# Spectral mixing plus gated MLP on one core: product 4 of gate and up joined over both position halves, and a last half block in a PSUM bank of its own

## The chip, the core and the metric

The kernel runs on one core of a Trainium2 chip. A core has TensorE (matrix products into PSUM, eight banks of 512 fp32 columns), VectorE and ScalarE (element by element), GpSimd and SyncE, whose queues here issue DMAs (called POOL and SP in the profile). The metric is the device time of one execution in microseconds, as the median of several runs.

## The reference

Two branches share the input `x` (2048 positions, 512 features) and are mixed by a gate per position:

```python
g = sigmoid((x * gate_w).sum(-1, keepdims=True))
a = Real(DFT_seq(DFT_hidden(x)))        # matrices given: Cr@(x@Wre.T) - Ci@(x@Wim.T)
gate = x @ W_gate; up = x @ W_up        # 512 -> 1792
b = (gate * (gate > 0) * up) @ W_down   # 1792 -> 512
return g * a + (1 - g) * b
```

All is fp32.

## The kernel before

**Precision.** Each fp32 operand is split into a high part (`h`: a ScalarE cast to fp32r) and a low part (`l`: a VectorE subtraction), and each product of tiles is three matmuls, low x high, high x low and high x high (`PARTS`). A matmul is 128x128 weights by 512 columns.

**Stages in order of time.**

1. *Gate/up.* The 14 column tiles of W_gate and W_up are taken in seven column pairs `c`, the positions in two halves `q`. For one `c` and `q` a two by two block product is done by seven products in place of eight (the products 1 to 7 of `LEFT`, `RIGHT`): sums of input blocks on either side, and sums of results. Each of the seven is 2 sides (gate and up, `i`) x 2 k x 3 parts = 12 matmuls, accumulated in PSUM bank pairs `x`, `m`, `y`, `t`. ReGLU makes `h` from them, which is written to HBM (`hd`). Pairs 0 and 1 of half 0 come first; pair 2 runs as two plain `Block`s; pairs 3 to 6 run as `Joined`: there product 2 of both halves together is done by another seven products of one k each (`JointX` makes its right sides once, `JointW` its left sides per pair, `jw`). Pairs 0 and 1 of half 1 are run between the spectral blocks.
2. *Spectral blocks*: x times the hidden DFT matrices, results `a` and sums `as` stored to HBM (`ad`).
3. *Down*, twice (`q` = 0, 1): h times W_down by seven products. `RAW` lists the (half, group of two pairs) whose forms of `h` are summed here (`made`) from four stored blocks; for the others seven forms are stored in stage 1 (`h_sums`) and read here.
4. *Sequence*: 26 products (`TURN`), each 4 parts x 12 matmuls, right sides from the sequence DFT matrices (`r`, `c`), left sides from `ad` (`l`, `w`). `SUMS` tells how operands are summed from others. Some right sums (`FORMED`) are made ahead into HBM (`td`): by DRAM-to-DRAM copies with an accumulating second copy, both issued by POOL (`form_stored`, paced by tokens), or by loads, VectorE sums and stores (`form_rights`, `form_lefts`). Results are summed in PSUM and in SBUF (`js`), gated and accumulated into the output.

**The order of work** is made by a planner at build time. Every step has a key: a time in units of one matmul (0.22667 us). TensorE's steps keep their order; for VectorE and ScalarE the planner takes due times (`due`) and a small model, and fixes one order for each engine; DMA issues stay in the order of their keys. SBUF is 51 units (`UNITS`) of 4 KB per partition, given out by the same plan. `LEAD`, `RAMP`, `FORM_LEAD` and `ahead` shift keys of preparation. `load` issues on SP, `store` and `accumulate` on POOL, and `put` is `load`. All instructions are issued at line 266, so the profile is read by tile names.

**The tail.** In the last turn the products of side `i` = 1, part 3 are done in two halves of 256 columns, both in the same bank; after each, `tail` multiplies by the gate, adds the value stored before, and SP stores the result:

```python
for i, cols, k in ((0, slice(N), 12), (1, HALVES[0], 3), (1, HALVES[1], 0)):
    z = o[:, i, cols]
    op(key - k, lambda z=z, i=i, cols=cols: E().vector.scalar_tensor_tensor(
        z, x[i][:, cols], float(sign), g[:, cols], op0=OP.mult, op1=OP.mult))
    op(key - k, lambda z=z, i=i, cols=cols: combine(z, z, v[:, i, cols], 1))
    op(key - k, lambda z=z, i=i, cols=cols: load(od[t, :, 2 * d + i, cols], z))
```

The functions that the change touches, and what calls them, with the line numbers of the profile:

Of the kernel before, what the change touches and what calls it, by code (L numbers as in the profile page):

```python
# [9 lines left out]
F32R = mybir.dt.float32r  # L10
# [10 lines left out]
UNITS = 51  # L21

# [34 lines left out]
FORMED = (16, 18, 19, 35, 37, 38)  # L57
# [211 lines left out]
class Plan:  # L269
# [47 lines left out]
    def due(self):  # L317

        last, n = {}, self.now
        for s in reversed(self.steps):  # L320
            if s.engine == "tensor" and s.key >= 0:
                n -= 1
            if s.engine == "tensor":
                last[s] = min(last.get(s, 1e9), n * self.MATMUL)
            elif s not in last or s.key > 0:
                last[s] = min(last.get(s, 1e9), (s.key + self.REST) * self.MATMUL)
            s.due = last[s] - (s.work + self.LANDING if s.name == "dma_start" else 0)
            for x in s.after:
                last[x] = min(last.get(x, 1e9), s.due - self.WAIT - (x.work if x.name != "dma_start" else 0))
# [91 lines left out]
def kernel(ctx: ExitStack, tc, xP, xG, wgu, wd, cr, ci, wri, gw, out):  # L421
# [189 lines left out]
    RAW = {(0, 1), (1, 2), (0, 0), (0, 3), (0, 2)}  # L611
# [97 lines left out]
    class Joined(Block):  # L709


        def __init__(self, q, w):
            super().__init__(q, w)
            self.u["11"] = buf("u11")
            if not q:
                self.s[1] = buf("s1")

        def run(self, joint=None):
            slots = {(5, 1): (5, 1), (6, 1): (6,), (3, 0): (3, 7), (3, 1): (2, 4)}
            for m, i in [(m, i) for m in (1, 5, 6) for i in range(2)] + [(3, 0), (7, 0), (3, 1), (7, 1), (4, 0), (4, 1)]:  # L720
# [5 lines left out]
                for y in slots.get((m, i), ()) if joint else ():  # L726
                    joint.step(y)
# [42 lines left out]

    class JointW:


        def __init__(self, w, x, key):
            self.w, self.x = w, x
            raw, s = buf("jws", [4, P]), w.raw[0]
            self.t = buf("jw", [2, 4, P], F32R)
            self.s = {y: buf(f"jv{y}", (N,)) for y in (1, 5, 6)}
            self.o = [buf(f"jo{q}") for q in range(2)]
            op(key - 30, lambda: combine(raw[:, 0], s[:, 1, 0, 1], s[:, 1, 1, 1], 1))  # L780
            op(key - 30, lambda: combine(raw[:, 2], s[:, 1, 0, 0], s[:, 1, 0, 1], -1))
            op(key - 29, lambda: combine(raw[:, 1], raw[:, 0], s[:, 1, 0, 0], -1))
            op(key - 28, lambda: combine(raw[:, 3], s[:, 1, 1, 0], raw[:, 1], -1))
            op(key - 24, lambda: E().scalar.copy(self.t[:, 0], raw.all))
            op(key - 20, lambda: E().vector.tensor_sub(self.t[:, 1], raw.all, f32(self.t[:, 0])))

        def left(self, y, a):
            if y in (1, 2, 4):
                return self.w.a[a][:, 1, int(y > 1), int(y == 4)]
            return self.t[:, a, {5: 0, 6: 1, 7: 2, 3: 3}[y]]  # L790
# [5 lines left out]
        def product(self, y):  # L796
            for n, (a, b) in enumerate(PARTS):
                mm(PAIRS["x"][int(y in (5, 3, 2))], self.left(y, a), self.x.x[y][:, b],
                   start=y in (1, 5, 2) and n == 0, stop=n == 2)

        def evac(self, y, key):
            Y, M = (PAIRS["x"][n] for n in range(2))
            s, o, e = self.s, self.o, E()
            if y in (1, 5, 6):
                op(key, lambda: e.scalar.copy(s[y].all, M if y == 5 else Y))
            elif y == 4:
                op(key, lambda: e.scalar.copy(o[0][:, 1], Y))
            else:
                q, i, ps, t = {3: (1, 0, M, 6), 7: (1, 1, Y, 5), 2: (0, 0, M, 1)}[y]
                op(key, lambda: e.vector.tensor_add(o[q][:, i], ps, s[t].all))  # L810
# [60 lines left out]
    class SpectralBlock:  # L871
# [47 lines left out]
        def out(self, f, key):  # L919
            for j in range(2):  # L920
                n = 2 * PLACE.index(2 * self.q + j)
                o = ad[f, n:n + 2, :, 2 * self.ih:2 * self.ih + 2].rearrange("x p t n -> p x t n")
                op(key, lambda o=o, j=j: store(o, self.o[f"{f + 1}{j + 1}"].all))
            part = {x: self.o[f"{f + 1}{PLACE[x // 2] % 2 + 1}"][:, x % 2] for x in range(8) if PLACE[x // 2] // 2 == self.q}
            mine = [v for v in DIRECT if GROUP[v] == self.q]
            for n, v in enumerate(mine):
                if n % 2 == 0:
                    s = buf("as", (2, 2, HD))
                p, q, sign = signed(*SUMS["l"][v - 8], SIGNS["l"], v)
                y = part[v] = s[:, n % 2]  # L930
                op(key + 2 + 4 * n, lambda y=y, p=part[p], q=part[q], sign=sign: combine(y, p, q, sign))
                op(key + 6 + 4 * n, lambda y=y, v=v: store(ad[f, v, :, 2 * self.ih:2 * self.ih + 2], y))
# [152 lines left out]
    def formed(side, blocks, trails, parts, first, last, source, name, shape):  # L1085
# [4 lines left out]
        for part, trail in chains:  # L1090
            old = None
            for x, v in trail:
                b = buf(name, shape)
                op(key - FORM_LEAD, lambda b=b, x=x, part=part: load(b.all, source(part, x)))
                if old:
                    a, o = old
                    p, q, s = signed(*SUMS[side][v - blocks], SIGNS[side], v)
                    p, q = (o, b) if p == a else (b, o)
                    op(key, lambda o=o, p=p, q=q, s=s: combine(o.all, p.all, q.all, s))
                    op(key + 5, lambda o=o, v=v, part=part: put(source(part, v), o.all))  # L1100
                old = x, b
                key += gap
# [32 lines left out]
    class Sequence:  # L1135
# [79 lines left out]
        def run(self):  # L1215
# [6 lines left out]
            for turn, product in enumerate(TURN):  # L1222
                (rv, rg), (lv, lg), (ov, og) = (SIDE[x][product] for x in "rlo")
                ps, fresh, sign = joins.begin(turn, ov, SIGNS["r"][rv] * rg * SIGNS["l"][lv] * lg * og)
                late = []
                for part in range(4):
                    c = self.split("c", (2, N), *r[turn, part], False)
                    if part % 2 == 0:
                        w = self.split("w", (4, HD), *l[turn, part], sign < 0)
                    if turn < len(TURN) - 1 or part < 2:  # L1230
                        for i in range(2):
                            pe(6, self.product, ps, w, c, part, fresh, i)
                    else:
                        late.append((w, c, part))
                for i, (w, c, part) in sorted(((i, x) for i in range(2) for x in late), key=lambda y: (y[0], y[1][2])):
                    if (i, part) == (1, 3):
                        for cols in HALVES:
                            pe(3, self.product, ps, w, c, part, fresh, i, cols)
                    else:
                        pe(6, self.product, ps, w, c, part, fresh, i)  # L1240
                joins.end(turn, ov)

        def product(self, ps, w, c, part, fresh, i, cols=slice(N)):
            hh = part % 2
            for k in range(2):
                for n, (a, b) in enumerate(PARTS):
                    mm(ps[i][:, cols], w[a][:, 2 * hh + k, i * P:(i + 1) * P], c[b][:, k, cols],
                       start=fresh and part == k == n == 0, stop=part == 3 and k == 1 and n == 2)

    class Joins:  # L1250


        def __init__(self, stage):
# [7 lines left out]
            self.place, self.free, self.late, self.turn = {}, [(Pair(n), -999) for n in range(4)], None, 0  # L1261

# [19 lines left out]
        def begin(self, turn, v, sign):  # L1282
# [6 lines left out]
            if fresh or kind == "s":  # L1289
                p, freed = self.free.pop(0)  # L1290
                if not fresh:
# [9 lines left out]
            return x, fresh, sign * s  # L1301

# [46 lines left out]
        def done(self, v):  # L1349
# [3 lines left out]
            g, key = buf("gg", (N,)), self.at(self.turn + 1)  # L1353
            row = gd[0, KD * t:KD * (t + 1)].rearrange("i p -> (i p)").partition_broadcast(P)
            op(key - 80, lambda: load(g.all, row))
# [12 lines left out]
        def tail(self, x, sign, t, d, g, key):  # L1368
            o, v = buf("z"), buf("v")
            op(key - 100, lambda: load(v.all, od[t, :, 2 * d:2 * d + 2]))  # L1370
            for i, cols, k in ((0, slice(N), 12), (1, HALVES[0], 3), (1, HALVES[1], 0)):
                z = o[:, i, cols]
                op(key - k, lambda z=z, i=i, cols=cols: E().vector.scalar_tensor_tensor(
                    z, x[i][:, cols], float(sign), g[:, cols], op0=OP.mult, op1=OP.mult))
                op(key - k, lambda z=z, i=i, cols=cols: combine(z, z, v[:, i, cols], 1))
                op(key - k, lambda z=z, i=i, cols=cols: load(od[t, :, 2 * d + i, cols], z))

# [87 lines left out]
    def prepared(c, ahead=74):  # L1465
# [4 lines left out]
    for c in range(2, NP):  # L1470
# [10 lines left out]
        else:  # L1481
            pair = [Joined(q, w) for q in range(2)]
# [30 lines left out]
    for n in range(2):  # L1513
# [64 lines left out]
```

## Time and profile before

| | |
|---|---|
| median of 3 runs | 770.4 us (769.77 to 770.6) |
| the profiled execution, its own time | 770.19 us |
| its span, first to last instruction | 768.4 us |
| TensorE busy | 762.5 us, 3360 matmuls |
| VectorE busy | 652.1 us |
| ScalarE busy | 407.1 us |
| mean granted TensorE clock | 0.999 |
| DMA packets, bytes | 60046, 190.16 MB |

Times in rows are microseconds from the start of the span unless marked ns. A timeline row gives start, duration, engine, line, operation, output tile `<-` input tiles, shape, count, and in brackets idle time before it and what ended it. A row of the stretches gives, per engine, busy time and number of instructions (PE, PE weight load, DVE, ACT, POOL), then the clock, the DMA engines' busy share and GB/s. A row of the groups gives total busy time and the mean of one in ns, then idle time before them. A DMA row gives count, KB each, and median us from issue to landing.

### The profile page before, as it was taken

To read this page: it belongs to the slowest core of one execution; us is meant where nothing else is said; L and a number is where in the kernel's file an instruction comes from. 1 tells how busy PE (TensorE), PEld (TensorE's weight loads), DVE (VectorE), ACT (ScalarE), POOL (GpSimd) and SP (SyncE) were. 2 spreads that over 40 slices of the span, in tenths; PEclk is the share of its full clock that TensorE was granted. 3 is DMA by queue.
4 is the path that set the end of the run, shared out by engine and by line. 5 is a ranking of instruction groups with operands and counts; after the bars stand their busy time and mean duration, and the time that the engine had idled before them with its cause. 6 is when DMAs were issued, how large, how long until landed. Compare 5 with 4: busy or idle time off the path is not lost.

```text
span 768.4 us, 9329 instructions
## 1 busy us (share of the span) xinstructions
PE 762.5 (99%) x3360; PEld 629.0 (82%) x3360; DVE 652.1 (85%) x714; ACT 407.1 (53%) x493; POOL 110.0 (14%) x163
## 2 busy tenths in 40 slices
PE   9999999999999999999999999999999999999997
PEld 7888888888888888888888888888888887888886
DVE  6999766738489784989998669999999999979984
ACT  6666444534445354555654535656675455826740
POOL 0122121111110332020000000022110110113020
PEclk9999999999999999999999999999999999999999
DMA  8376897866897989787349898899995997999885
GB/s 320 121 237 158 259 271 212 238 182 189 256 296 270 358 330 333 261 283 260 111 165 348 285 391 253 247 245 228 263 267 186 258 258 251 239 238 282 263 178 109
DMA packets 60046, 190.16 MB, mean 247 GB/s; under 512 B 6752, under 2 KB 7264, under 8 KB 60000
## 3 DMA queue, kind: packets, MB, share of 16 engines
q1 hardware_dynamic: 41776, 124.03, 44.8%
q0 software_dynamic: 18224, 65.54, 37.6%
q8 instruction: 26, 0.43, 0.2%
q14 instruction: 20, 0.16, 0.1%
HBM read 143.65 MB, written 66.86 MB: 274 GB/s over the span
## 4 chain that ended last, share of the span: by engine, by line
PE 96%; DVE 3%; issue 1%; DVEq 0%
PE ps L266 96%; DVE cl L266 1%; DVE wl L266 0%; DVE r L266 0%; DVE js L266 0%; DVE z L266 0%; DVE ps L266 0%; DVE l L266 0%; DVEq L266 0%
## 5 line engine op out<-in xcount | busy, mean ns | idle before, releaser
L266 PE MATMUL ps<-ch,wl 128*128 128x512 f32 x418 | 162.4, 389 | 0.1
L266 PE MATMUL ps<-cl,wh 128*128 128x512 f32 x418 | 162.3, 388 | 0.2 <-DVE cl L266 0.2
L266 PE MATMUL ps<-ch,wh 128*128 128x512 f32 x418 | 162.2, 388 | 0.0
L266 ACT CAST ch<-r 128x1024 fp32r<-128x1024 f32 x104 | 105.9, 1050 | 95.1 <-DVE r L266 67.7
L266 DVE TENSOR_TENSOR cl<-r,ch 128x1024 fp32r<-128x1024 f32 x104 | 124.6, 1221 | 0.4
L266 PEld LDWEIGHTS ps<-ch,wl 128*128 128x128 f32 x418 | 78.5, 188 | 17.0 <-DVE js L266 0.9
L266 PEld LDWEIGHTS ps<-cl,wh 128*128 128x128 f32 x418 | 78.5, 188 | 16.5 <-DVE cl L266 0.6
L266 PEld LDWEIGHTS ps<-ch,wh 128*128 128x128 f32 x418 | 78.5, 188 | 16.3
L266 PE MATMUL ps<-ch,ll 128*128 128x512 f32 x196 | 76.2, 389 | 0.0
L266 PE MATMUL ps<-cl,lh 128*128 128x512 f32 x196 | 76.2, 389 | 0.0
L266 PE MATMUL ps<-ch,lh 128*128 128x512 f32 x196 | 76.2, 389 | 0.0
L266 ACT CAST ch<-hr 128x1024 fp32r<-128x1024 f32 (+1 forms) x56 | 51.3, 943 | 34.8 <-DVE hr L266 20.5
L266 DVE TENSOR_TENSOR cl<-hr,ch 128x1024 fp32r<-128x1024 f32 (+1 forms) x56 | 59.2, 1087 | 9.8 <-ACT ch L266 9.7
L266 ACT COPY s<-ps 128x1024 f32<-128x1024 f32 (+1 forms) x48 | 41.8, 872 | 45.1 <-PE ps L266 44.1
L266 DVE TENSOR_TENSOR u<-ps,s 128x1024 f32<-128x1024 f32 x28 | 34.2, 1220 | 15.6 <-PE ps L266 8.8
L266 DVE TENSOR_TENSOR wl<-l,wh 128x1024 fp32r<-128x1024 f32 x38 | 46.2, 1220 | 0.0
L266 ACT ACTIVATE ps<-ps 128x512 f32<-128x512 f32 (+1 forms) x30 | 23.4, 781 | 43.0 <-PE ps L266 42.2
L266 ACT CAST wh<-l 128x1024 fp32r<-128x1024 f32 x38 | 39.5, 1048 | 11.6 <-DVE l L266 11.2
L266 PE MATMUL ps<-xh,wb0l 128*128 128x512 f32 x112 | 43.7, 390 | 0.0
L266 PE MATMUL ps<-xh,wb0h 128*128 128x512 f32 x112 | 43.6, 389 | 0.0
L266 PE MATMUL ps<-xl,wb0h 128*128 128x512 f32 x112 | 43.6, 389 | 0.0
L266 PE MATMUL ps<-xh,wb1l 128*128 128x512 f32 x112 | 43.6, 389 | 0.0
(147 smaller groups left out, 1504.5 us busy)
## 6 DMA issues: line engine op xcount, KB each, us to landing
l<-ad SPq DMA_DIRECT2D x32, 512.0 KB, 6.8
hr<-hd SPq DMA_DIRECT2D x30, 512.0 KB, 5.4
td<-cr POOLq DMA_DIRECT2D x20, 512.0 KB, 6.0
td<-ci POOLq DMA_DIRECT2D x20, 512.0 KB, 6.3
r<-td SPq DMA_DIRECT2D x20, 512.0 KB, 8.0
wr<-wgu SPq DMA_DIRECT2D x16, 512.0 KB, 8.3
ad<-a POOLq DMA_DIRECT2D x16, 512.0 KB, 6.2
r<-cr SPq DMA_DIRECT2D x16, 512.0 KB, 7.5
```

Of the source, the lines that this page charges most:

```text
L266: getattr(getattr(nc, self.engine), self.name)(*map(ap, self.a), **{k: ap(x) for k, x in self.k.items()})
```

## The change

Four things change.

- Product 4 of column pairs 4, 5 and 6 (`FOURS = 4`) is taken for both halves by seven products, as product 2 was: `JointFour` makes its right sides once, a second `JointW` (with `m=4`) its left sides per pair. The block 21 is then the contents of bank pair `y` minus the joined result (`last`). In half 1, products 6 and 7 use bank pair `t`, and the order of the products changes.
- The last turn's second side is split into two halves of columns for parts 2 and 3, and the last half goes to a spare bank, to which ScalarE copies what was accumulated. For that half, the accumulated block and the right operands are multiplied by the gate, and the stored value is added, before the matmuls (`gate_early`), so that only a copy is left, which ScalarE makes and stores by a DMA that it issues itself (`tail_gated`).
- Right sum 17 is formed ahead (`FORMED`, `form_rights([17], ...)`); the times of the other forming steps, `RAW`, and several leads are new.
- Spectral outputs are stored through SP (`put`), and the formed sums through POOL (`store`). In `due` a matmul counts by its columns.

```diff
+FOURS, FOUR_KEY, FOUR_W = 4, -140, 30
-FORMED = (16, 18, 19, 35, 37, 38)
+FORMED = (16, 17, 18, 19, 35, 37, 38)
-LEAD = {'r': {'load': 44, 'sum': 52, 'sums': 6, 'draws': 30, 'hi': 42, 'lo': 34}, 'l': {'load': 40, 'sum': 62, 'sums': 8, 'draws': 40, 'hi': 55, 'lo': 38}}
-RAMP = 40
-FORM_LEAD = 60
+LEAD = {'r': {'load': 44, 'sum': 60, 'sums': 6, 'draws': 30, 'hi': 42, 'lo': 26}, 'l': {'load': 38, 'sum': 62, 'sums': 6, 'draws': 40, 'hi': 55, 'lo': 34}}
+RAMP = 80
+FORM_LEAD = 46
...
             if s.engine == "tensor" and s.key >= 0:
-                n -= 1
+                n -= s.writes[0].size() / N
...
-    RAW = {(0, 1), (1, 2), (0, 0), (0, 3), (0, 2)}
+    RAW = {(0, 1), (0, 0), (1, 1), (0, 3), (0, 2), (1, 0), (1, 3)}
...
     class Joined(Block):
+            if four and q:
+                self.banks = {**PAIRS, "y": PAIRS["t"]}
...
+            order = [(3, 0), (7, 0), (3, 1), (7, 1), (4, 0), (4, 1)]
+            fours = {}
+            if self.four:
+                slots = {(5, 1): (5, 1), (6, 1): (6,), (7, 0): (3, 7), (3, 0): (2, 4)}
+                fours = {(6, 0): (5, 1), (7, 0): (6,), (7, 1): (3, 7), (3, 0): (2, 4)}
+                order = [(7, 0), (7, 1), (3, 0), (3, 1)]
+            for m, i in [(m, i) for m in (1, 5, 6) for i in range(2)] + order:
                 pe(6, self.product, m, i)
-                if m in (6, 7):
+                if m == 6 or m == 7 and not self.four:
                     self.half(m, i, plan.now)
...
+                for j, some in ((self.four, fours), (joint, slots)) if joint else ():
+                    for y in some.get((m, i), ()):
+                        j.step(y)
+                        if j is self.four and y == 4:
+                            self.last(plan.now)
+                if self.four and not joint and (m, i) == (7, 1):
+                    self.last(plan.now)
+
+        def last(self, key):
+            u, y, o = self.u["21"], self.banks["y"], self.four.o[self.q]
+            op(key + 1, lambda: E().vector.tensor_sub(u.all, y.all, o.all))
+            op(key + 2, lambda: E().vector.scalar_tensor_tensor(
+                self.h[1][:, 0], u[:, 0], 0.0, u[:, 1], op0=OP.max, op1=OP.mult))
...
+    class JointFour:
+        def __init__(self, key):
+            a, b = (X[q, 4][2] for q in range(2))
+            for n, (y, src, f) in enumerate(((5, t5, (b[:, 0], a[:, 0])), (6, t6, (b[:, 1], t5)),
+                                             (7, t7, (b[:, 1], b[:, 0])), (4, t4, (a[:, 1], t6)))):
+                x = self.x[y] = buf(f"kx{y}", dtype=F32R)
+                op(key + 12 * n, lambda src=src, f=f: combine(src, *f, -1))
+                op(key + 12 * n + 4, lambda x=x, src=src: E().scalar.copy(x[:, 0], src))
+                op(key + 12 * n + 8, lambda x=x, src=src: E().vector.tensor_sub(x[:, 1], src, f32(x[:, 0])))
...
     class JointW:
-        def __init__(self, w, x, key):
+        def __init__(self, w, x, key, m=2):
+            raw, s = buf("jws", [4, P]), w.raw[0][:, 1] if m == 2 else w.raw[1][:, 0]
+            self.bank = PAIRS["x" if m == 2 else "t"]
...
-                op(key, lambda o=o, j=j: store(o, self.o[f"{f + 1}{j + 1}"].all))
+                op(key, lambda o=o, j=j: put(o, self.o[f"{f + 1}{j + 1}"].all))
...
-                    op(key + 5, lambda o=o, v=v, part=part: put(source(part, v), o.all))
+                    op(key + 5, lambda o=o, v=v, part=part: store(source(part, v), o.all))
...
+                if turn == len(TURN) - 1:
+                    order[4:] = [(2, 0, slice(N)), (3, 0, slice(N)), *((part, 1, cols) for cols in HALVES for part in (2, 3))]
...
+                    if joins.gated:
+                        op(hi - 1, lambda raw=raw: E().vector.tensor_mul(raw[:, :, HALVES[1]], raw[:, :, HALVES[1]], joins.wide))
...
+                    if (turn, part, i) == (len(TURN) - 1, 2, 0):
+                        joins.spare = joins.free[0][0]
+                        op(plan.now, lambda: E().scalar.copy(ps8[:, joins.spare.n + 1, HALVES[1]], ps8[:, ps.n + 1, HALVES[1]]))
...
+        def gate_early(self, v, x, s, key):
+            op(key - 100, lambda: load(self.v.all, od[t, :, 2 * d:2 * d + 2]))
+            y, z = x[:, :, half], self.v[:, :, half]
+            op(key, lambda: E().vector.tensor_mul(y, y, self.wide))
+            op(key, lambda: combine(y, y, z, s * FLIP_T[t]))
...
+        def tail_gated(self, x, sign, t, d, key):
+            for i, n, k in ((0, 0, 12), (0, 1, 12), (1, 0, 6), (1, 1, 0)):
+                z, y = o[:, i, cols], ps8[:, (x if k else self.spare).n + i, cols]
+                if n:
+                    op(key - k, lambda z=z, y=y: E().scalar.activation(z, y, AF.Copy, scale=float(sign)))
+                else:
+                    op(key - k, lambda z=z, y=y, cols=cols: E().vector.scalar_tensor_tensor(
+                        z, y, float(sign), self.g[:, cols], op0=OP.mult, op1=OP.mult))
+                    op(key - k, lambda z=z, i=i, cols=cols: combine(z, z, self.v[:, i, cols], 1))
+                if i or n:
+                    issue = plan.scalar.dma_start if i and n else load
...
-    form_stored([37, 18, 16, 19], 156, 18)
-    form_stored([35], 788, 30)
-    form_rights([38], 784, 1330)
+    form_stored([16, 37, 18], 150, 11)
+    form_stored([19], 693, 21)
+    form_rights([38], 906, 1367)
+    form_rights([17], 1221, 1632)
-    def prepared(c, ahead=74):
+    def prepared(c, ahead=82):
...
+            if c == FOURS:
+                four_x = JointFour(plan.now + FOUR_KEY)
+            four = c >= FOURS and JointW(w, four_x, plan.now + FOUR_W, 4)
+            pair = [Joined(q, w, four) for q in range(2)]
...
+    form_stored([35], plan.now + 112, 19)
     Down(lw, 0)
-    form_lefts([8], plan.now + -141, plan.now + 157)
+    form_lefts([8], plan.now + -292, plan.now + -92)
```

More of the change, by code (lines that the diff above doesn't have):

```diff
@@ L771 @@
     class JointW:
-        def __init__(self, w, x, key):
-            self.w, self.x = w, x
-            raw, s = buf("jws", [4, P]), w.raw[0]
+        def __init__(self, w, x, key, m=2):
+            self.w, self.x, self.m = w, x, m
+            raw, s = buf("jws", [4, P]), w.raw[0][:, 1] if m == 2 else w.raw[1][:, 0]
             self.t = buf("jw", [2, 4, P], F32R)
-            self.s = {y: buf(f"jv{y}", (N,)) for y in (1, 5, 6)}
+            two, one = buf("jv"), buf("jv6", (N,))
+            self.s = {1: two[:, 0], 5: two[:, 1], 6: one[:]}
@@ L797, in product @@
             for n, (a, b) in enumerate(PARTS):
-                mm(PAIRS["x"][int(y in (5, 3, 2))], self.left(y, a), self.x.x[y][:, b],
+                mm(self.bank[int(y in (5, 3, 2))], self.left(y, a), self.x.right(y, b),
                    start=y in (1, 5, 2) and n == 0, stop=n == 2)
         def evac(self, y, key):
-            Y, M = (PAIRS["x"][n] for n in range(2))
+            Y, M = (self.bank[n] for n in range(2))
             s, o, e = self.s, self.o, E()
             if y in (1, 5, 6):
-                op(key, lambda: e.scalar.copy(s[y].all, M if y == 5 else Y))
+                op(key, lambda: e.scalar.copy(s[y], M if y == 5 else Y))
             elif y == 4:
@@ L809, in evac @@
                 q, i, ps, t = {3: (1, 0, M, 6), 7: (1, 1, Y, 5), 2: (0, 0, M, 1)}[y]
[L810 removed]
+                op(key, lambda: e.vector.tensor_add(o[q][:, i], ps, s[t]))
     def gate(t, key):
@@ L1290, in begin @@
                 p, freed = self.free.pop(0)
+                if not fresh and turn == len(TURN) - 1:
+                    self.gate_early(v, x, s, max(self.at(turn) - 18, freed + .5))
                 if not fresh:
@@ L1352, in done @@
             sign *= FLIP_T[t]
-            g, key = buf("gg", (N,)), self.at(self.turn + 1)
-            row = gd[0, KD * t:KD * (t + 1)].rearrange("i p -> (i p)").partition_broadcast(P)
-            op(key - 80, lambda: load(g.all, row))
+            key = self.at(self.turn + 1)
+            if self.gated:
+                return self.tail_gated(x, sign, t, d, key)
+            g = buf("gg", (N,))
+            self.row(t, g, key - 80)
             wide = g.all.unsqueeze(1).to_broadcast([P, 2, N])
```

76 lines of the change are left out of this document (46 added, 30 removed).

## The prediction

> **What bounds the kernel now.** I read the page's busy shares first, then the chain of waits, then the list of what TensorE waited for.
>
> ```profile
> span 768.4 us, 9329 instructions
> PE 762.5 (99%) x3360; PEld 629.0 (82%) x3360; DVE 652.1 (85%) x714; ACT 407.1 (53%) x493; POOL 110.0 (14%) x163
> ```
> ```profile
> 4.80 523.27 PE ps L266 x2302
> ...
> 531.64 89.84 PE ps L266 x395
> ...
> 644.75 118.81 PE ps L266 x528
> ...
> 763.59 0.44 DVE z L266
> ```
> ```profile
> PE ps L266 <- PEq L1571: 0.8, 1, 0.8
> PE ps L266 <- DVE cl L266: 0.2, 1, 0.2
> ```
>
> TensorE is busy 99% of the span and waited 1.0 us in all. The chain is matmuls from 4.80 on, save one detour over VectorE that ends at 531.64 and one that ends at 644.75, and VectorE's four tail operations from 763.59. So the time is the number of matmuls times their spacing, plus 4.8 us of head, a few tenths of gaps and a tail. The execution with these rows took 770.19 us: 1.79 above its span, and 0.21 under the median of 770.4.
>
> ```profile
> 119.45 0.39 PE L266 MATMUL ps<-xh,wd 128*128 128x512 f32 x1
> 119.68 0.39 PE L266 MATMUL ps<-xh,wal 128*128 128x512 f32 x1
> ...
> 531.08 0.39 PE L266 MATMUL ps<-ch,wl 128*128 128x512 f32 x1
> 531.64 0.50 PE L266 MATMUL ps<-cl,wh 128*128 128x512 f32 x1 [0.18 <-DVE cl L266]
> 531.98 0.40 PE L266 MATMUL ps<-ch,wh 128*128 128x512 f32 x1
> ...
> 761.96 0.28 PE L266 MATMUL ps<-ch,wl 128*128 128x256 f32 x1
> ...
> 763.27 0.28 PE L266 MATMUL ps<-ch,wh 128*128 128x256 f32 x1
> ```
>
> Here the starts count, not the durations (matmuls overlap): 0.227 us apart at 512 columns. The twelve of 256 columns start from 761.96 to 763.27, so 0.119 apart. The matmul at 119.68 is the first of column pair 4.
>
> **Part 1: product 4 joined.** In each of column pairs 4, 5 and 6, product 4 leaves both position halves: 2 halves x 2 sides x 2 k x 3 parts = 24 matmuls go, 7 x 3 = 21 come. Nine fewer in all, 9 x 0.227 = **-2.04 us**, all on the path. The work beside them:
>
> ```profile
> 114.00:151.00 37.00, 37.00 (x165) 30.63 (x164) 25.57 (x37) 17.10 (x30) 7.17 (x14) 1.00 0.82 225
> 151.00:189.00 38.00, 38.00 (x169) 31.49 (x168) 23.35 (x32) 16.98 (x27) 4.08 (x8) 1.00 0.70 198
> 189.00:226.00 37.00, 37.00 (x165) 30.61 (x165) 23.97 (x27) 16.32 (x25) 5.70 (x9) 1.00 0.84 257
> ```
> ```profile
> L266 DVE TENSOR_TENSOR u<-ps,s 128x1024 f32<-128x1024 f32 x16 | 19.5, 1221 | 9.7 <-PE ps L266 8.8 <-ACT ps L266 0.9
> L266 ACT COPY s<-ps 128x1024 f32<-128x1024 f32 x12 | 12.2, 1015 | 20.0 <-PE ps L266 20.0
> L266 ACT COPY s<-ps 128x512 f32<-128x512 f32 x16 | 9.4, 588 | 6.8 <-PE ps L266 6.8
> L266 DVE TENSOR_TENSOR jo<-ps,jv 128x512 f32<-128x512 f32 x12 | 7.9, 686 | 20.0 <-PE ps L266 10.1 <-issue 9.9
> L266 DVE TENSOR_TENSOR jws<-wr 128x128 f32<-128x128 f32 x8 | 2.3, 285 | 0.0
> L266 ACT CAST wb0h<-ws 128x1024 fp32r<-128x1024 f32 x4 | 4.2, 1053 | 2.6 <-DVE ws L266 2.6
> ```
>
> VectorE gets, per pair, two `u21` subtractions of 1.22, three bank additions and one weight split of 0.69 and four weight sums of 0.285: 6.3 us, 19 for three pairs. The group (1, 2), pairs 4 and 5 of position half 1, leaves the list RAW, so its sums are made here again: 8 x 0.69 = 5.5. Busy time of VectorE (fifth figure of the first three rows) goes from 72.9 to 97.4 of 112 us, 87%. ScalarE loses six operations of 0.59 per pair and gains five. The right side of the new product, made once (four differences, four splits, 5.5 us of VectorE), falls near 90 us. On average all of it fits beside the matmuls. What can stall TensorE is the hand-over of PSUM banks, which comes sooner than before in three places:
>
> ```profile
> 173.62 0.62 PE L266 MATMUL ps<-jx,wah 128*128 128x512 f32 x2
> ```
> ```profile
> 174.28 0.59 ACT L266 COPY jo<-ps 128x512 f32<-128x512 f32 x1 [2.08 <-PE ps L266]
> ```
>
> - The second of these two matmuls starts at 173.85 and ends the joined product 2. ScalarE reads its bank 0.43 us later for 0.59, done 1.01 after that start. Six matmuls, where there were eighteen, now lie before position half 1 reuses the bank: 0.227 + 6 x 0.227 = 1.59 after that start. 0.57 is spare; a cast of 1.05 begun just ahead costs up to 0.5.
> - The sum `u12` must have read bank pair m before half 1's product 5: 13 spacings, 2.95 us, where it had 31. It needs 0.43 + 1.22, so 1.3 is spare: one VectorE operation ahead fits, a second costs up to 1.1.
> - Between steps 3, 7 and 2, 4 of the new product lie nine matmuls: 10 spacings, 2.27, for 0.43 + 0.69. 1.15 is spare.
>
> Bounds: 0 if both engines come at once, 3 x 0.5 + 3 x 1.1 = 4.8 if they come late in half 0 of every pair. I take **+0.45**, near the low end, since the rows show both engines idle, waiting for TensorE, before most such reads. A gain is excluded: there is no gap in this stage to win.
>
> **Part 2: the tail.**
>
> ```profile
> 763.59 0.42 DVE L266 SCALAR_TENSOR_TENSOR z<-ps,gg 128x256 f32<-128x256 f32 x1 [1.37 <-PE ps L266]
> ```
> ```profile
> 762.24 3.38 SPq L266 DMA_DIRECT2D out<-z  x3
> ```
> ```profile
> out<-z POOLq DMA_DIRECT2D x4, 512.0 KB, 5.9
> ...
> out<-z SPq DMA_DIRECT2D x2, 128.0 KB, 1.9
> ```
>
> The operation of the first quarter block was held 1.37 us, to the last matmul, though its own six matmuls were over: both quarters share a bank. Four operations of 0.42 follow that matmul, and the third store is issued at about 765.29 (the three issues end at 765.62, one takes 0.33): 2.02 after the last matmul's start. With a bank of its own the first quarter is worked off under twelve half-width matmuls (1.43 us) and stored about 0.2 before the last one starts. Left behind it are 0.32 of reaction, one ScalarE copy (588 ns at 512 columns, 1015 at 1024: about 374 at 256) and the issue, 0.75 together: **-1.27**. The second half-width group costs 6 x (2 x 0.119 - 0.227) = **+0.07**.
>
> No row has a store issued by ScalarE. The nearest are SP's landing of 1.9 and POOL's of 5.9, so the term lies between -1.27 and +2.7. I take SP's, the same plain 128 KB; POOL's accumulate and are four times larger. The Trainium skill ("DMA: Bandwidth & Descriptors", section "SWDGE vs HWDGE vs iDMA") says that a DMA issued from ScalarE takes the hardware path just as one from SP does; by it the term is -1.27, by POOL's path +2.7. No row here shows which holds.
>
> ```profile
> 748.69 1.22 DVE L266 TENSOR_TENSOR cl<-r,ch 128x1024 fp32r<-128x1024 f32 x1
> ```
> ```profile
> 752.66 0.39 PE L266 MATMUL ps<-cl,wh 128*128 128x512 f32 x1
> ```
>
> Gating ahead puts six VectorE operations of 512 elements (0.69) into the last two turns. The last turn's first `cl` is done at 749.91 and first read at 752.66: 2.75 spare, against two new operations on the accumulated block and one on that operand, 2.1. I take zero; up to 1.4 if further ones queue ahead. ScalarE's copy to the spare bank has 12 matmuls, 2.7 us, over it.
>
> **Part 3: what is moved and paced anew.**
>
> ```profile
> 38.80:98.70 59.90, 59.90 (x266) 49.61 (x265) 52.27 (x69) 34.45 (x52) 13.17 (x23) 1.00 0.79 220
> ...
> 411.00:478.00 67.00, 67.00 (x297) 55.50 (x296) 52.41 (x50) 32.24 (x35) 1.76 (x2) 1.00 0.90 324
> 453.00:531.00 78.00, 78.00 (x346) 64.59 (x345) 77.74 (x70) 46.07 (x49) 11.15 (x13) 1.00 0.92 253
> ```
> ```profile
> q0 software_dynamic: 18224, 65.54, 37.6%
> ```
> ```profile
> 93.12 6.63 SPq L266 DMA_DIRECT2D wr<-wgu  x2
> ```
> ```profile
> 112.16 0.69 DVE L266 TENSOR_TENSOR ws<-wr 128x512 f32<-128x512 f32 x1
> ```
> ```profile
> DMA to landing us min/median/max: 3.1/7.6/13.5
> ```
> ```profile
> SPq L266 <- PE ps L266: 214.0, 72, 10.9
> ```
>
> Right sum 17 is formed ahead: four sums of 1.22 leave VectorE just before the Sequence, in a stretch where it is busy 77.74 of 78 us and at whose end TensorE has its gap at 531. Against them stand four raw sums of 0.69 (group (1, 3)). 2.1 us net come free against a gap of (0.56 - 0.23) + (0.34 - 0.23) = 0.45, so I let it go: **-0.45**. The detour that ends at 644.75 is late next and keeps its price. The new leads and the longer ramp may open others: bounds -0.45 to +3.
>
> At no cost, with the cover: sum 17's eight loads on SP, four sums and four stores (now on POOL) between 280 and 375 us, and `lefts` in the first Down, under matmuls that wait for nothing there; raw forms, 7.6 us more of sums in the second Down, where VectorE idles 14.6 of 67 us, and 8.3 less before it; 44 spectral stores that move from POOL to SP, 0.33 each there, in front of loads that lead their use by 20 us and more. With a cover gone each costs its own duration, 0.3 to 1.2.
>
> DRAM copies now come every 11 plan units (one unit is a matmul's 0.227), 2.49 us for 0.524 MB: 210 GB/s, where that queue moves 65.54 MB in 37.6% of 768.4 us, 227 GB/s. That is 93% of the DMA engines from 39 to 99 us, 57% before, beside 0.79 - 0.57 = 22% of others: some 9 us of backlog, hidden unless weights come late.
>
> Sum: 770.19 - 2.04 + 0.45 - 1.27 + 0.07 - 0.45 = 766.95; at the median's level **767.2**.
>
> **The rivals.** *Weights late (the slower side).* SP's loads wait mostly for buffers that TensorE still reads (214 us), and four right parts and up to six smaller buffers now take their place among the 51 units. Pair 4's second weight load went out near 99.4 and was used at 112.16, 5.2 after a median landing of 7.6; two sums, a cast and a split (3.7) end at 115.9 and are read two products after 119.68, at 122.4: 6.5 more. From 11.7 us of added delay on, each pair stalls; 2 us beyond it in three pairs gives **773.2**. For it: 93% of the DMA and 87% of VectorE. Against it: the lead. The same page of the Trainium skill, section "Queues, rings and completion order", says that each DMA engine takes turns between the queues that have work; then a full copy queue halves the weights' rate, 7.6 becomes at most 15, and the lead still holds. No row here shows the turns singly.
>
> *Hand-offs late:* 3.9 in place of 0.45, **770.6**. VectorE at 87% speaks for it, the idle time before its reads against. *The Sequence falls out worse:* new gaps of 2.5 before `cl`, **769.7**; the detours show that VectorE has no reserve there, the four sums less speak against. *The tail does not shorten:* the quarter is held as before, 768.5, or ScalarE's store lands like POOL's, 771.2; nothing in the trace excludes the second.
>
> **Chances.** Forecast 0.66, hand-offs 0.12, weights 0.09, Sequence 0.08, tail 0.05. A measurement here tells about 0.2%, 1.5 us, from no change: 768.9 to 771.9 is "same". Faster: 0.66 + 0.03 + 0.02 + 0.02 (the mild ends of hand-offs, Sequence and tail) = 0.73. Slower: weights 0.08, hand-offs 0.02, Sequence 0.01. Same: the remaining 0.16. The forecast alone spans 766.0 to 768.8 (hand-offs at 0 and the gap at 644 gone, to hand-offs and gaps of 2 us). The range goes on to 770.8, past the centre of the late hand-offs; it leaves out the weights and the far ends.
>
> **What would show it.** 3357 matmuls; spacing 0.227 without a gap from 119 to 229; two `u21` sums of 1.22 per pair there; the last matmul's start near 761; the last store issued about 0.75 after it and landing in 1.9; no gap near 531. The prediction is wrong if TensorE waits for readers of `ps` or for weight splits between 119 and 229, if `cl` gaps grow after 480, or if the last landing is well over 1.9.

## The result: 778.25 us, 1.06% above the kernel before

The changed kernel took 778.25 us in the median (778.1 to 778.58, four runs), the kernel before 770.09 beside it: a ratio of 1.0106 (95% interval 1.0089 to 1.0124). The forecast was 767.2, and at most 770.8. The profiled execution took 778.11 us, with a span of 776.3. One execution of run 5's kernel (1290 us) and one of the kernel before (1999 us) fell in a slow state and are left out of what follows.

From the page of the changed kernel, the span and the busy times:

```profile
span 776.3 us, 9373 instructions
PE 762.7 (98%) x3357; PEld 627.8 (81%) x3357; DVE 675.3 (87%) x752; ACT 409.5 (53%) x497; POOL 99.2 (13%) x129
```

There are 3357 matmuls, as forecast. What TensorE waited for:

```profile
PE ps L267 <- ACT jv L267: 5.5, 1, 5.5
PE ps L267 <- DVE cl L267: 0.8, 1, 0.8
```

One wait of 5.5 us is new. The chain of waits (start, duration, what; pieces under 0.1 us are left out) has it in its place:

```profile
86.58 12.92 DMA hd<-h
99.58 0.59 ACT jv L267
100.22 47.49 PE ps L267 x201
147.73 0.70 DVE jo L267
148.52 1.24 DVE u L267
149.84 0.59 ACT jo L267
150.47 34.36 PE ps L267 x150
...
187.59 505.44 PE ps L267 x2226
...
711.77 1.24 DVE cl L267
713.05 57.36 PE ps L267 x263
770.43 0.38 ACT z L267
```

Three things are new here. A store of `h` to HBM (`hd`) is issued at 86.58 and lands 12.92 us later; only then does ScalarE copy a joined result out of PSUM into `jv`, and only then does TensorE go on. Twice, at 150.47 and 187.59, TensorE is released by ScalarE's copy `jo`, which waited for VectorE's `u`. And the gap that stood at 531 is gone (one piece of matmuls from 187.59 to 693.05), but there is one before 713.05.

The copy reads PSUM alone, so it can wait for this store only because of where it writes: `jv` takes over a buffer that the stored `h` held. The same stop in the timeline of ScalarE and then of TensorE:

```profile
99.58 0.58 ACT L267 COPY jv<-ps 128x512 f32<-128x512 f32 x1 [6.01 <-DMA hd<-h]
```
```profile
93.86 0.84 PE L267 MATMUL ps<-jx,jw 128*128 128x512 f32 x3
100.22 1.65 PE L267 MATMUL ps<-jx,jw 128*128 128x512 f32 x3 [5.51 <-ACT jv L267]
101.66 0.63 PE L267 MATMUL ps<-xh,wb1l 128*128 128x512 f32 x1
102.09 0.63 PE L267 MATMUL ps<-xl,wb1h 128*128 128x512 f32 x1
...
103.74 0.40 PE L267 MATMUL ps<-xh,wb1h 128*128 128x512 f32 x1
103.98 0.40 PE L267 MATMUL ps<-xh,wb1l 128*128 128x512 f32 x1
```

The stop costs more than its length: after it the matmuls start 0.43 apart (101.66, 102.09) in place of 0.227 until about 103.7. 5.67 us are lost standing and 1.76 in the slow matmuls, 7.43 together.

Why the store took so long: the stretches before (first two rows) and after (the other three), with the DMA engines' busy share as the last figure but one.

```profile
40.00:76.00 36.00, 36.00 (x161) 29.80 (x160) 35.53 (x43) 23.45 (x35) 8.41 (x13) 1.00 0.75 205
76.00:92.00 16.00, 16.00 (x72) 13.26 (x71) 13.68 (x22) 8.11 (x14) 3.93 (x8) 1.00 0.76 234
```
```profile
40.00:76.00 36.00, 36.00 (x161) 29.80 (x160) 35.41 (x43) 23.34 (x37) 12.75 (x21) 1.00 0.99 275
76.00:92.00 16.00, 16.00 (x72) 13.27 (x71) 13.10 (x21) 8.84 (x14) 5.76 (x10) 1.00 1.01 238
92.00:114.00 22.00, 16.49 (x66) 13.16 (x66) 11.83 (x16) 5.63 (x10) 0.82 (x1) 0.84 0.70 202
```

From 40 to 92 us the DMA engines are full (0.99, 1.01) where they were at three quarters. Under them the stores to `hd` landed later. The landing times (min/median/max) of the stores issued between 40 and 115 us, before and after:

```profile
DMA to landing us min/median/max: 2.0/3.7/8.3
```
```profile
DMA to landing us min/median/max: 2.3/7.6/16.7
```

The store of 86.58 is not the worst of them: the three issued right behind it took 13.6 to 16.7 us and held nothing up. The tail, from the timelines of VectorE, GpSimd and ScalarE, and the row of the last store among the DMA issues:

```profile
764.33 1.22 DVE L267 SCALAR_TENSOR_TENSOR z<-ps,gg 128x1024 f32<-128x1024 f32 x1
```
```profile
765.84 0.85 POOL L267 DMA_DIRECT2D out<-z  x1 [9.15 <-DVE z L267]
```
```profile
770.43 0.38 ACT L267 ACTIVATE z<-ps 128x256 f32<-128x256 f32 x1 [2.48 <-PE ps L267]
770.84 0.38 ACTq L267 DMA_DIRECT2D out<-z  x1
```
```profile
out<-z ACTq DMA_DIRECT2D x1, 128.0 KB, 2.2
```

The last matmul starts at 770.11. ScalarE's copy and store do what was forecast: issued at 770.84, landed at about 773.0. But the span ends 6.16 us after that matmul, where it was 5.12 before. GpSimd's last accumulating store is issued at 765.84 (before at 754.16, 9.1 us ahead of the last matmul, now 4.3), because VectorE makes its `z` at 764.33, behind the operations of the gating ahead and the last operands `cl`, two of which it preceded in the kernel before. Which of the change's parts moved it there was not tried singly. GpSimd's closing drain, an instruction that the trace holds and these views leave out, runs 9.67 us from there, to 775.49, and the kernel's end waits for it.

The whole difference of 7.9 us, as the sum of what the matmuls' starts are apart beyond their ideal spacing:

| term | forecast | measured |
|---|---|---|
| fewer matmuls, second half-width group | -1.97 | -1.97 |
| stop at 100 us | 0 | +7.43 |
| hand-overs, 110 to 240 us | +0.45 | +1.04 |
| Sequence: 531, 580 to 680, 713 | -0.45 | -0.47 - 0.28 + 1.08 |
| tail | -1.27 | +1.04 |
| start of the kernel, to 40 us | 0 | +0.03 |

### The profile page after: what moved, and what is told of

The parts are those of the page before. It is cut to its first block, busy times and chain, and to the rows that moved or that the text cites. A ratio compares the mean times of both kernels' runs of the same rounds, so it can differ in the third digit from the quotient of the medians.

```text
span 776.3 us, 9373 instructions
## 1 busy us (share of the span) xinstructions
PE 762.7 (98%) x3357; PEld 627.8 (81%) x3357; DVE 675.3 (87%) x752; ACT 409.5 (53%) x497; POOL 99.2 (13%) x129
## 4 chain that ended last, share of the span: by engine, by line
PE 91%; DVE 4%; DMA 2%; ACT 1%; issue 1%; SPq 0%; ACTq 0%; DVEq 0%
PE ps L267 91%; DMA hd<-h 2%; DMA x<-xP 1%; DVE cl L267 1%; DVE u L267 1%; DVE r L267 1%; ACT ch L267 0%; DVE ws L267 0%; DVE h L267 0%; SPq L267 0%; DVE jo L267 0%; DVE js L267 0%; ACT jo L267 0%; DVE ps L267 0%; ACT xh L267 0%
## 5 line engine op out<-in xcount | busy, mean ns | idle before, releaser
L267 PE MATMUL ps<-cl,wh 128*128 128x512 f32 (+1 forms) x420 | 162.8, 388 | 0.8 <-DVE cl L267 0.8
L267 PE MATMUL ps<-ch,wl 128*128 128x512 f32 (+1 forms) x420 | 162.7, 387 | 0.0
L267 PE MATMUL ps<-ch,wh 128*128 128x512 f32 (+1 forms) x420 | 162.6, 387 | 0.0
L267 ACT CAST wh<-l 128x1024 fp32r<-128x1024 f32 x38 | 39.5, 1049 | 10.1 <-DVE l L267 8.8
L267 PE MATMUL ps<-xl,wb1h 128*128 128x512 f32 x112 | 44.0, 393 | 0.0
L267 PE MATMUL ps<-xh,wb1h 128*128 128x512 f32 x112 | 43.9, 392 | 0.0
```

The costliest lines, as they stand in the source:

```text
L267: getattr(getattr(nc, self.engine), self.name)(*map(ap, self.a), **{k: ap(x) for k, x in self.k.items()})
```

## The experiments

Short names used below: *the copies* are the DRAM-to-DRAM copies of `form_stored` in the gate/up stage; *the right parts* are `kx`, made once by `JointFour`.

**1. The copies spread out again.**

```
-    form_stored([16, 37, 18], 150, 11)
+    form_stored([16, 37, 18], 150, 18)
```

> The changed kernel with one number changed: the DRAM-to-DRAM copies of sums 16, 37 and 18 start every 18 plan units, as before the change, and not every 11. Three theories on the 5.7 us stop at 100 us and the 1.8 us of half-speed matmuls after it. A (both needed): a store of h lands 12.9 us after its issue because the dense copies fill the DMA engines, and a ScalarE copy has to wait for that landing because no other buffer is free; with the copies spread the store lands in 6 to 8 us, the stop shrinks to 0 to 2 us: 771 to 773 us. B (the copies alone, whatever the buffers): the stop goes altogether, 770.8. C (the buffers alone): the stop stays, 778.

770.93 us (770.62 to 772.47); ratio to before 1.0015 (1.0005 to 1.0024). Stretches and the landing times of the stores to `hd` between 40 and 115 us in this kernel:

```profile
76.00:92.00 16.00, 16.00 (x72) 13.24 (x72) 13.23 (x22) 8.86 (x16) 4.39 (x8) 1.00 0.76 235
92.00:114.00 22.00, 22.00 (x99) 18.22 (x98) 15.80 (x24) 10.14 (x17) 4.14 (x8) 1.00 0.89 232
```
```profile
DMA to landing us min/median/max: 2.1/3.3/8.2
```

TensorE is busy 22.00 of 22 us where it stood. Spreading the copies is enough to take the stop away, so theory C is out: the store that stopped TensorE, issued at 86.65 here, lands after 2.84 us, where theory A had expected 6 to 8. Left are the tail (6.18) and the smaller gaps.

**2. The copies dense, the right parts later.**

```
-FOURS, FOUR_KEY, FOUR_W = 4, -140, 30
+FOURS, FOUR_KEY, FOUR_W = 4, -60, 30
```

> The changed kernel with one number changed: the four right parts of the new product are made 60 plan units (13.6 us) ahead of column pair 4 and not 140 (31.7 us), so that they hold no buffers at 88 to 100 us; the copies stay every 11 units. A (both needed): the copy into jv takes another buffer, which has long been free, the stop at 100 us goes although the store still lands late: 770.5 to 771.5. C (buffers alone): the same. B (the copies alone): something at 90 to 105 us still waits for a landing of 10 us or more: 775 to 778.

771.36 us (770.67 to 772.6); ratio 1.0014 (1.0004 to 1.0023). The stop is gone too, with the DMA engines as full as in the changed kernel (1.01 from 40 to 92 us) and the store as late: issued at 86.73, it lands after 12.75 us, and TensorE does not wait for it. That rules theory B out. A gap of 0.47 at 120.5 is new. The stop takes both: full DMA engines make the store late, and the right parts, made 18 us earlier than here, leave `jv` no buffer but the one that store keeps. Either mend alone removes the stop.

**3. Before, with the copies dense.**

```
-    form_stored([37, 18, 16, 19], 156, 18)
+    form_stored([37, 18, 16, 19], 156, 11)
```

> The kernel before with one number changed: its copies come every 11 plan units and not every 18. A (both needed): there the buffers had 3 to 5 us to spare between the landing that the plan expects and the next use, so stores land late but TensorE stops for 0 to 1.5 us: 770 to 771.5. B (the copies alone): a stop of 4 us or more near 90 to 110 us: 774 or more. C (buffers alone): 770.

773.07 us (772.78 to 775.95); ratio 1.0045 (1.0027 to 1.0064). Its longest wait in sum:

```profile
PE ps L266 <- ACT ps L266: 3.2, 3, 1.7
```

Dense copies cost about 3 us in the median without any part of product 4. The stops lie elsewhere, at 118, 121.5 and 200 us. The larger estimate, 774 and more, was not reached and the smaller, up to 1.5 us, was exceeded. The profiled run, of 775.95, was the longest of its four; its stops, 6.0 us in all between 110 and 240, are more than the median's. In front of those at 118 and 121.5 stand these pieces of the chain and this wait of VectorE, in front of those at 196 and 200 this wait of ScalarE:

```profile
88.52 18.74 DMA hd<-hs
...
107.76 10.70 DMA wr<-wgu
```
```profile
115.98 0.29 DVE L266 TENSOR_TENSOR jws<-wr 128x128 f32<-128x128 f32 x1 [11.20 <-DMA wr<-wgu]
```
```profile
194.33 1.05 ACT L266 CAST wb1h<-ws 128x1024 fp32r<-128x1024 f32 x1 [2.71 <-DMA hd<-h]
```

Here too the landing of a store is at the root. The first, of 18.74 us, held two weight loads back, which went out at 107.31 and 107.76 where before they went out at 93.12 and 99.41: in this run the weights did come late. The second held back ScalarE's cast of weights. The comparison with run 2, where dense copies cost 0.4 us (771.36 against run 1's 770.93), is not an even one: this list makes four sums and that of the change three, and the DMA engines stay full to 124 us (a busy share of 1.06 from 114 to 124, where the changed kernel has 0.21).

**4. The last accumulated sum gated earlier** (in `due`, for `z` of the last turns).

```
-                last[s] = min(last.get(s, 1e9), (s.key + self.REST) * self.MATMUL)
+                rest = 20 if s.key > self.now - 60 and any(x.base.name == "z" for x in s.writes) else self.REST
+                last[s] = min(last.get(s, 1e9), (s.key + rest) * self.MATMUL)
```

> The changed kernel with the due time of the last two gated results z (before the tail) set 9 us earlier, so that VectorE makes them ahead of the last operands and POOL issues its last accumulating store at about 761 us and not at 765.84. Theory P: what ends the span is POOL's drain, which ends 9.7 us after that store is issued; the end moves by 2 to 2.4 us, to where SP's waits end: 775.9 to 776.3 us. Rival Q: ScalarE's own store and its queue set the end: no change, 778.2, with the last gap of 2.4 us still there. Rival R: the earlier z holds up the last operands and TensorE stops for 1 us: 777.

776.9 us (775.94 to 777.28); ratio 1.0084 (1.0067 to 1.0101). The forecast of 775.9 to 776.3 was missed, because VectorE puts the sum only one operation further ahead. The store follows:

```profile
764.45 0.85 POOL L267 DMA_DIRECT2D out<-z  x1 [7.94 <-DVE z L267]
```

Counted from the last matmul (769.92) the store went out 1.2 us earlier than in the changed kernel, and the tail is 1.1 shorter (5.07). The end moves with that store, as the theory of the drain has it; the step was smaller than asked for.

**5. All three mended**: pace 18, `FOUR_KEY` -60, and `rest = 0` in the line of run 4.

> The changed kernel with three numbers changed: copies every 18 plan units, right parts 60 units ahead, and the last gated results z due 13.6 us earlier, so that POOL issues its last store some 5 us earlier against the last matmul (in the run with 9 us it had moved by 1.2 us only). Theory P (POOL's drain of 9.7 us after its last store sets the end): the end now follows SP's waits, about 3.9 us after the last matmul's start in place of 6.1, so 770.9 less 2.2: 768.4 to 769.0. Rival Q (ScalarE's queue sets the end): 770.9, with 6 us after the last matmul's start.

768.9 us (768.32 to 770.15); ratio 0.9972 (0.9958 to 0.9987): a little below before, and clear of it.

```profile
753.85 0.85 POOL L267 DMA_DIRECT2D out<-z  x1 [4.23 <-DVE z L267]
```

The store goes out 9.2 us ahead of the last matmul (763.09), GpSimd's drain is over at 763.6, and the end follows ScalarE's store: 3.62 us after the last matmul, 1.50 less than before. No stop is left at 100 us.

**6. The mended kernel without the joined product 4** (`FOURS = 9`: no pair takes it).

> The mended kernel without the joined product 4 (column pairs 4 to 6 as before the change; copies every 18 units, early z, all else as changed). It has nine matmuls more, 2.04 us, and none of the gaps that came with the joined product: 0.33 at two starts of position half 1 and about 0.1 to 0.4 elsewhere, some 1.0 us in all. If the joined product is worth its matmuls less those gaps, this kernel takes 0.8 to 1.3 us more than the mended one: 769.5 to 770. Rival: the joined product's VectorE work and buffers cost as much as it saves, the two are equal within 0.3.

769.18 us (769.0 to 769.75); ratio 0.9974 (0.9961 to 0.9987). Nine matmuls more, no hand-over gap between 110 and 240. Its span is 0.7 above run 5's, its median 0.3; the two intervals cover each other, so a difference of 0.3 is not shown. The 0.8 to 1.3 that were expected are missed; the rival, equal within 0.3, fits the medians. Of the 2.04 us that the seven products save, the hand-overs of run 5 take 1.05 back.

**7. The mended kernel with `LEAD` and `RAMP` of before.**

> The mended kernel with LEAD and RAMP of before. With the new ones the Sequence has gaps of 1.35 us in all, 1.03 of them near 706; with the old ones the kernel before had 0.94, of which 0.45 (at 531) should go with right sum 17 formed ahead. If the new leads made the gap near 706: 0.4 to 0.9 less than the mended one, near 768. Rival: the old leads with the new operations (gating ahead, sum 17) open gaps as large elsewhere: equal or up to 1 us more.

769.5 us (768.45 to 771.49); ratio 0.998 (0.9964 to 0.9995). The gap near 706 (1.14 in run 5) is gone and one of 2.3 near 524 has come, at the end of this piece of the chain:

```profile
506.61 11.28 DMA r<-td
...
523.50 0.49 ACT js L267
524.03 3.03 PE ps L267 x12
```

The new leads are no loss on balance: they move a gap and halve it.

**8. The mended kernel without the gating ahead** (the call of `gate_early` left out; the last half bank stays apart, VectorE gates and adds, SyncE stores).

> The mended kernel (copies every 18, right parts at -60, last accumulated sum gated at once) without the gating ahead: the last half block keeps its bank apart, but is gated and added to by VectorE after the last matmul and stored through SyncE. Theory G (the gating ahead and ScalarE's copy are what shorten the tail): two VectorE operations of 0.42 come back behind the last matmul in place of a copy of 0.38, so the stretch from the last matmul's start to the end goes from 3.6 to about 4.1 to 4.3 us (5.12 before, with four such operations). Theory B (the bank apart alone does it, the store by ScalarE is no faster): 3.6 to 3.8. If gpsimd's last accumulating store still set the end, 6 or more.

768.99 us in one run. From the last matmul (763.12) to the end 4.06. Its VectorE:

```profile
763.44 0.42 DVE L267 SCALAR_TENSOR_TENSOR z<-ps,gg 128x256 f32<-128x256 f32 x1 [0.48 <-PE ps L267]
763.90 0.42 DVE L267 TENSOR_TENSOR z<-z,v 128x256 f32<-128x256 f32 x1
```

Two operations where before had four (5.12) and run 5 has one copy (3.62). By these single executions the bank apart is worth 1.06 and the gating ahead 0.44; of the 1.06, 0.30 lie behind the last landing (0.91 us from there to the end, where before had 1.21). This is near theory G and not B.

**9. The mended kernel, the last store issued by SyncE.**

```
-                    issue = plan.scalar.dma_start if i and n else load
+                    issue = load
```

> The mended kernel with the last 128 KB store issued by SyncE in place of ScalarE; the copy stays on ScalarE. Prediction's reading (the two ways land alike): the stretch from the last matmul's start to the end stays at 3.6 us within 0.1, one hand-over between engines more. Rival (a store from ScalarE is itself quicker or slower): a difference of 0.3 us or more.

768.49 us in one run; 3.56 from the last matmul to the end, run 5's 3.62 within 0.1. Which of the two engines issues the store makes no difference.

**10. The mended kernel with the ramp of before, `RAMP = 40`.**

> The mended kernel with the ramp of the leads at the start of the Sequence back at 40, the leads themselves as in the change. It splits the run with both taken back, where a gap of about 1 us near 706 went and one of 2.3 us near 524 came. Theory R (the ramp covers the start, the leads make the late gap): gaps near 524 of 1.5 to 2.5 us and near 706 of about 1 us, 770 to 771 us. Theory L (the leads do both): no gap near 524, about 1 us near 706, the time of the mended kernel, 768.9.

768.23 us (767.72 to 770.42); ratio 0.9961 (0.9943 to 0.9979), the lowest median of all, with an interval that overlaps run 5's. There is no gap near 524 and one of 1.0 near 708: so the leads, not the ramp, decide between the two, as theory L has it. The profiled run was the slowest of the eight (770.42); 1.7 us of that went at 172.7 and 0.75 at 190.8. Its ScalarE at the first of these:

```profile
172.04 0.58 ACT L267 COPY jv<-ps 128x512 f32<-128x512 f32 x1 [2.77 <-DMA hd<-hs]
```

It is the wait of 100 us once more, in small: `jv` waits for a buffer until a store from it has landed, here 6.25 us after its issue.

## Why the prediction was wrong

**The step that failed: the copies' backlog, "hidden unless weights come late".** The forecast found the load (93% and 9 us of backlog; measured 99%), and gave the late weights 0.09 as a rival. It asked only who waits for loads. The weights were not late in the changed kernel: no matmul waited for them, and the weight loads issued between 40 and 115 us landed as follows, before and after:

```profile
DMA to landing us min/median/max: 6.6/7.7/8.4
```
```profile
DMA to landing us min/median/max: 3.3/6.9/10.1
```

By turns between the queues, which the Trainium skill ("DMA: Bandwidth & Descriptors", section "Queues, rings and completion order") describes, the forecast let a full copy queue stretch the loads' 7.6 to at most 15. The loads stayed inside that bound: the two issued under the copies took 8.9 and 10.1 us. The stores had no such bound put on them; the one that decided took 12.92, and no run tells whether turns between queues or something else made it so.

What came late was a store, and a store's landing is also a release: its source buffer comes free only then. The forecast had the other half in hand too ("four right parts and up to six smaller buffers now take their place among the 51 units"), and put it down to weight loads waiting for buffers, not to results of matmuls that must leave PSUM. Runs 1 and 2 show that the two halves together make the stop, and run 3 that in the kernel before, too, late stores stop TensorE when the copies are dense. Of the 11.1 us that the time lies above the forecast, 5.67 are the wait itself and 1.76 the slow matmuls behind it, both in place of a zero; the tail has 2.3 more.

**The tail: term right, cover overlooked.** ScalarE's store landed in 2.2 us, near SyncE's 1.9 and not GpSimd's 5.9. The Trainium skill ("DMA: Bandwidth & Descriptors", section "SWDGE vs HWDGE vs iDMA") says that the two engines take the same hardware path; run 9 agrees, with 3.56 against 3.62. In the changed kernel that landing came 2.92 us after the start of the last matmul, against 3.91 before: -0.99 for a forecast of -1.27, and -1.20 in run 5, where the store took 1.98. SyncE, which then waits for every queue, was done at 3.06 against 4.35. That this difference, -1.29, is the forecast's number is in part luck: 0.30 of it is that SyncE has fewer waits left behind the last landing, which the forecast did not count. But the forecast put the gating ahead at zero, since `cl` had 2.75 us to spare, and did not ask what else stood behind those operations on VectorE: the last accumulated `z`, whose store and drain GpSimd then ended last. Run 5 gave -1.50 with the drain out of the way, the same 0.30 in it.

**Hand-overs: place right, size off, cause different.** +1.04 where 0.45 was taken, within the bounds of 0 to 4.8. At the reuse of the joined product's bank, the first of the three places named, TensorE loses 0.33 in pair 4 and 0.33 in pair 5. Another 0.11 and 0.13 go at 195.9 and 232.8, where product 7 of half 1 adds to a bank that ScalarE has just copied, a place that the forecast did not name; the rest is in spacings a little above 0.227 behind these gaps. Ahead of the first place ScalarE's timeline in the changed kernel has

```profile
149.84 0.58 ACT L267 COPY jo<-ps 128x512 f32<-128x512 f32 x1 [1.52 <-DVE u L267]
```

The spare of 0.57 was worked out as though ScalarE waited for TensorE alone. It waits 1.52 us for VectorE's `u` (148.52, 1.24 long), the new `u21`, which reads product 4's `jo`; the copy writes product 2's. That one buffer is passed from the one to the other fits these rows, but only the wait itself is shown.

**The Sequence.** The gap at 531 went, -0.47 for -0.45. The new leads opened one near 713, +1.03, inside the stated bound of +3. Run 7 shows that it is the other side of the same choice.

**Right at zero:** sum 17's loads and sums, the moved stores and the raw forms. From 187.59 to 693.05 the changed kernel's matmuls run in one piece.

**The matmuls:** 3357, -2.04, but by run 6 joining product 4 leaves 0.7 us of it by the span and 0.3 by the median, which is within the spread.

**The rivals.** *Weights late* named 773.2 and was the right alarm on the wrong victim; its time was 5 us short. In run 3 its victim was hit, by the same late landing of a store. None named the drain.

What stays open is a part of GpSimd's drain. From the issue of its last store it took 7.36 us in the kernel before and 7.35 in run 3, and 9.66 to 11.43 in the changed kernel and those made from it. Counted from that store's landing the figures are nearly constant: it ends 1.97 us later in the kernel before and in run 3, and 4.33 to 4.34 later in the ten others. So the landing, of 5.3 to 7.1 us, makes the spread among the ten, and a fixed 2.37 us came with the change. Run 8, which has neither the gating ahead nor ScalarE's store, has the 4.33 too, and so has run 6 without the joined product 4, so these are not the reason; what is, no run tells.

## What to carry to other kernels

Where DMA queues get fuller, list the stores too: a buffer is free when its store has landed, so look for the engine operation that writes that buffer next, and ask whether TensorE waits for it. A step put ahead on a busy engine moves everything behind it; follow that to the last instruction of every queue, since the end here was set by whichever queue was done last, and a tail is shortened only if the next-latest end moves too. A price of zero needs two names: who reads next what is moved, and who writes next into the buffer that it leaves.

## What the runs showed of the hardware

- *Matmuls after a stop.* After 5.5 us without work they started 0.427 us apart, and at 0.227 again from about 103.7, 3.5 us after the restart; the granted clock was 0.50 from 96.84 to 103.67 and 1.00 around. The Trainium skill ("TensorE: Matmul & The Clock Gate", section "Part 1: The HAM clock gate (the "warmup" mystery)") puts the rate at half until about 3.4 us of sustained work are done; this trace agrees. This stop cost a third more than it lasted. After run 7's stop of 2.06 us the matmuls were back at 0.227 from the second start on.
- *Stores under full DMA engines.* The 512 KB store of `h` at 86.58 took 12.92 us to land, and the same store 12.75 in run 2 and 2.84 in run 1, where the copies are spread. Over all stores to `hd` between 40 and 115 us, median and longest were twice those before (7.6 and 16.7 against 3.7 and 8.3).
- *GpSimd's drain* at the end of the program ends 1.97 us after its last store has landed in two of the kernels here and 4.33 to 4.34 after it in ten, and in the changed kernel it was the last thing that the program waited for.
